# Retention and feed-forward kernel: the values of chunks 0 to 3 loaded through ScalarE's DMA queue, two casts placed earlier, and the last output block in one piece

## The chip, the core and the metric

The kernel runs on one core of a Trainium2 chip. The metric is the device time of one execution in microseconds (us), shorter being better. The core's engines are TensorE (PE in the profile, with its weight loads as PEld), VectorE (DVE), ScalarE (ACT), GpSimd (POOL) and SyncE (SP). Each works through its own list of instructions in order, and they meet through semaphores. Transfers between HBM and the on-chip memory are issued by an engine and carried out by 16 DMA engines.

## The reference

A retention layer with state (4 batches, 8 heads, 768 positions, head size 64) is followed by a feed-forward part without a nonlinearity. All inputs and the output are float32.

```python
gamma = 1.0 - 2.0 ** (-5.0 - np.arange(H))
for t in range(S):
    state = gamma * state + einsum('bhd,bhe->bhde', k[:, :, t], v[:, :, t])
    y[:, :, t] = scale * einsum('bhd,bhde->bhe', q[:, :, t], state)
x = y.transpose(0, 2, 1, 3).reshape(3072, 512)
h = ((x @ w1) * (x @ w2)) @ w3
out = h @ w_out
```

## The kernel before

**Tiling.** The 768 positions of a batch are cut into 6 chunks of 128, so there are 24 chunks, n = 0 to 23. A chunk's work is `casts(n)` on GpSimd (queries of a pair of chunks, keys, and values scaled into the buffer VP[n % 3], to float16), `transposes(n)` (keys transposed, on TensorE for early chunks), `scores(n)`, `kv(n)` (the state's update: a product on TensorE, an addition on VectorE, a decay on GpSimd at line 391) and `outputs(n)`, which uses the masked scores, VP and the state that `kv(n-1)` left. Its result is a piece of x. The feed-forward part works on blocks of at most 256 tokens of x: units "a" and "b" (x by w1 and w2) and "o" (the product by W3O). W3O = w3 by w_out is computed once at the start, since nothing stands between the two.

**Order of the work.** It is written by hand. A prologue loads w3 and w_out, transposes w3 block by block and builds W3O (lines 558 to 592), works on chunks 0 and 1 between (lines 583 to 598), casts w1 and w2 to float16 (lines 595 to 603, 631, 632), does the first block of tokens (lines 625 to 653), then chunks 2 and 3 (lines 666 to 682). From then on `step(n)` handles one chunk, and `fill.pull` puts feed-forward units between its parts (lines 519 to 540, 684 to 688). `step` calls `casts(n + 2)` ahead of the scores for n of 6 or more and behind `kv(n)` for n = 4 and 5.

**Loads.** All of them are issued by SyncE, through `dma_in` (line 62), in the order of lines 115 to 125: eight blocks for w3 and w_out, four more blocks of w3, the queries of chunks 0 and 1, keys and values of chunk 0, of chunk 1, four blocks of w1, four of w2, queries, keys and values of chunks 2 and 3, and the same of 4 and 5. A weight block or a pair's queries has 512 KB, a chunk's keys or values 256 KB in pieces of 256 bytes. Below, q0 stands for the queries of chunks 0 and 1, q2 for those of chunks 2 and 3, q4 for those of 4 and 5, k0 and v0 for the keys and values of chunk 0, and so on.

**Completion semaphores.** The framework has eight semaphores for such transfers (DMAHW0 to DMAHW7). It hands them out in turn, in the order in which the program's text issues the transfers, whichever engine issues them. Before an engine issues a transfer, it waits until the transfer that had the same semaphore last, eight places back in the text, has landed. Here is how the list of SyncE's instructions of this kernel shows it (rows 8 to 15 of the list):

```
8 L62 DMACopy stg<-in_moe_w_out_dram 128x1024
9 L62 DMACopy stg<-in_moe_w_dram 128x1024 [waits DMAHW0_49]
...
13 L62 DMACopy q_111<-in_q_dram 128x8x128 [waits DMAHW4_49]
14 L62 DMACopy k_113<-in_k_dram 128x8x64 [waits DMAHW5_49]
15 L62 DMACopy v_115<-in_v_dram 128x8x64 [waits DMAHW6_49]
```

**Stores.** `o_unit` (line 448) makes a block of 128 rows of the output: eight matmuls of 512 columns, one copy on ScalarE, one store by SyncE. The last block is made by `last_o_unit` (line 462) in two halves of 256 columns, each with its own copy and store.

Of the kernel before, what the change touches and what calls it, by code (L numbers as in the profile page):

```python
# [9 lines left out]
FP = mybir.dt.float32  # L10
HP = mybir.dt.float16
AF = mybir.ActivationFunctionType
# [6 lines left out]
def kernel(  # L19
# [11 lines left out]
    nc = tc.nc  # L31
    B, H, S, D = q.shape
    C = 128
    WST = 12
    NCH = S // C
    NSTEP = B * NCH
    NTOK = B * S
    DT0 = 8
    NP = H // 2
    DM = 512  # L40
    DFF = 1024

    final_scale = 1.0 / D
# [6 lines left out]
    ld = ctx.enter_context(tc.tile_pool(name="ld", bufs=6))  # L50
    att = ctx.enter_context(tc.tile_pool(name="att", bufs=2))
    fsb = ctx.enter_context(tc.tile_pool(name="fsb", bufs=2))
# [3 lines left out]
    ps_f = ctx.enter_context(tc.tile_pool(name="ps_f", bufs=3, space=PSUM))  # L56
# [4 lines left out]
    def dma_in(dst, src):  # L61
        nc.sync.dma_start(dst, src)  # L62

    chunk_in = {}
    q_in = {}

    def load_chunk(n):
        if n >= NSTEP:
            return
        b, c = divmod(n, NCH)  # L70
        tiles = []
        if c % 2 == 0:

            t = ld.tile([128, 2 * 512], FP, tag="q64", name="q64", bufs=3)
            dma_in(
                t[:, :].rearrange("p (h x) -> p h x", x=2 * D),
                q[b, :, c * C : (c + 2) * C, :].rearrange("h (p t) d -> p h (t d)", t=2),
            )
            q_in[n // 2] = t
        for nm, src in (("k", k), ("v", v)):  # L80
            t = ld.tile([128, 512], FP, tag=nm + "32", name=nm + "32")
            dma_in(
                t[:, :].rearrange("p (h d) -> p h d", d=D),
                src[b, :, c * C : (c + 1) * C, :].rearrange("h i d -> i h d"),
            )
            tiles.append(t)
        chunk_in[n] = tiles

    def new_stage():
# [56 lines left out]
    for h in range(H):  # L146
# [7 lines left out]
        out=keep[:, :], in_=keep[:, :], compare_op=mybir.AluOpType.is_ge, fill=0.0,  # L154
# [20 lines left out]
    for h in range(H):  # L175
        p, r = h // 2, (h % 2) * 64
# [9 lines left out]
    W3O = [wpool.tile([128, DM], HP, name=f"w3o_{i}") for i in range(8)]  # L186
# [3 lines left out]
    def cast_to(dst, src, on_dve):  # L190
        if on_dve:
            nc.vector.tensor_copy(dst, src)  # L192
        else:
            nc.scalar.copy(dst, src)  # L194
# [4 lines left out]
    def cast_w3(key, st):  # L199
        t = att.tile([128, 1024], HP, tag="w3h", name="w3h", bufs=4)  # L200
        cast_to(t[:, :], st[:, :], False)
        W3h[key] = t
# [22 lines left out]
    def w3_transpose(f):  # L225
        src, ps = w3_bank(f, f)
        for g in range(8):
            c0 = (g // 2) * 256 + g % 2
            nc.tensor.transpose(
                ps[:, g * 128 : (g + 1) * 128], src[:, c0 : c0 + 255 : 2], ident16[:, :]  # L230
            )
        w3_back(f, ps)

    def w3_mm_columns(i, acc, between=None):
        t = w3t.pop(("c", i))
        for f in range(4):
            if f == 2 and between:
                between()
            for r in range(2):
                g = f * 2 + r  # L240
                nc.tensor.matmul(
                    acc[f], lhsT=t[:, g * 128 : (g + 1) * 128], rhs=WO[i][:, r, :],
                    start=(i == 0 and r == 0), stop=(i == 3 and r == 1),
                )
            if i == 3:
                cast_to(W3O[f][:, :], acc[f], f < 3)
# [17 lines left out]
    def casts(n):  # L264
        if n >= NSTEP:
            return
        k32, v32 = chunk_in.pop(n)
        if n % 2 == 0:
            q16 = att.tile([128, 1024], HP, tag="q16", name="q16")
            nc.gpsimd.tensor_copy(  # L270
                q16[:, :].rearrange("i (t h d) -> i h t d", t=2, d=D),
                q_in.pop(n // 2)[:, :].rearrange("i (h t d) -> i h t d", t=2, d=D),
            )
            q16s[n // 2] = q16
        k16 = att.tile([128, 512], HP, tag="k16", name="k16", bufs=3)
        nc.gpsimd.tensor_copy(k16[:, :], k32[:, :])  # L276
        vp = VP[n % 3]

        for r in range(2):
            nc.gpsimd.tensor_tensor(  # L280
                vp[:, :, r, r * 64 : r * 64 + 64],
                v32[:, :].rearrange("j (p s e) -> j p s e", s=2, e=64)[:, :, r, :],
                VS[:, :].rearrange("j (p s) -> j p s", s=2)[:, :, r].unsqueeze(2).broadcast_to((128, NP, 64)),
                MULT,
            )
        k16s[n] = k16
# [30 lines left out]
    def dma_transposes(n):  # L317

        if n < DT0 or n >= NSTEP:
            return  # L320
        kT = att.tile([128, NP, 128], HP, tag="kT", name="kT", bufs=2)
        nc.sync.dma_start_transpose(kT[:, :, :], k16s[n][:, :])
        kTs[n] = kT
        if n % 2 == 0:
            qT = att.tile([128, 2, NP, 128], HP, tag="qTd", name="qTd", bufs=2)
            nc.sync.dma_start_transpose(
                qT[:, :, :, :].rearrange("p t a i -> p (t a) i"), q16s.pop(n // 2)[:, :]
            )
            qTd[n // 2] = qT
# [23 lines left out]
    def scores(n):  # L353
        kp = KP[n % 2]
        am = att.tile([128, NP, 2, 128], HP, tag="am", name="am")
        for half in range(2):
            ps = ps_at.tile([128, 2, 2, 128], FP, tag=f"psA{half}", name=f"psA{half}")
            for i in range(2):
                p = half * 2 + i
                for r in range(2):  # L360
                    nc.tensor.matmul(  # L361
                        ps[:, i, r, :], lhsT=kp[:, p, r, :], rhs=queries(n, p), start=True, stop=True
                    )
            nc.vector.tensor_tensor(  # L364
                am[:, half * 2 : half * 2 + 2, :, :].rearrange("j p s i -> j (p s) i"),
                ps[:, :, :, :].rearrange("j p s i -> j (p s) i"),
                keep[:, :].unsqueeze(1).broadcast_to((128, 4, 128)),
                MULT,
            )
        ATs[n] = am  # L370
# [44 lines left out]
    class Ffn:  # L415
# [43 lines left out]
            r0 = self.tok0 + tb * 128  # L459
            nc.sync.dma_start(out[r0 : r0 + 128, :], osb[:, :])  # L460

        def last_o_unit(self, tb):

            osb = fsb.tile([128, DM], FP, tag="osb", name="osb", bufs=3)
            r0 = self.tok0 + tb * 128
            for c in range(2):
                cs = slice(c * 256, c * 256 + 256)
                psO = ps_f.tile([128, 256], FP, tag="psF", name="psO")
                for f in range(8):
                    nc.tensor.matmul(  # L470
                        psO[:, :], lhsT=self.HT[:, f, tb * 128 : (tb + 1) * 128], rhs=W3O[f][:, cs],
                        start=(f == 0), stop=(f == 7),
                    )
                nc.scalar.activation(osb[:, cs], psO[:, :], AF.Copy, scale=final_scale)
                nc.sync.dma_start(out[r0 : r0 + 128, cs], osb[:, cs])

        def ab_units(self):
            need, m = self.tok0 + self.width, TB // self.width
            units = []
            for f in range(0, 8, m):  # L480
                units += [(need, 0.43, lambda f=f: self.a_unit(f)), (need, 0.43, lambda f=f: self.b_unit(f))]
            return units
# [32 lines left out]
    fill = Queue()  # L515
# [3 lines left out]
    def step(n):  # L519

        ready = n * C
        share = fill.available(ready) / (2 - n % 2)
        if n >= DT0 - 2:
            casts(n + 2)
        scores(n)
        fill.pull(share * 0.25, ready)
        t_new = kv(n)
        if n < DT0 - 2:
            casts(n + 2)
        dma_transposes(n + 2)  # L530
        if n == DT0 - 2:
            load_chunk(n + 4)
        if n % 2:
            q_transposes((n + 1) // 2)
        if n != 5:
            fill.pull(share * 0.25, ready)
        outputs(n)
        Tst[0] = t_new
        transposes(n + 1)
        fill.pull(share * (0.75 if n == 5 else 0.5), ready)  # L540

    def cast_w(W, st, d, on_dve):
        cast_to(W[d][:, :], st[d][:, :], on_dve)
# [29 lines left out]
    cast_wo(3)  # L573
    cast_w3(4, w3_st[4])
    cast_w3(5, w3_st[5])
    w3_mm_columns(3, acc)
    w3_transpose(4)
    w3_transpose(5)
# [19 lines left out]
    Tst[0] = kv(1)  # L598
    cast_w(W1, w1_st, 1, False)
    cast_w(W1, w1_st, 2, False)  # L600
    cast_w(W1, w1_st, 3, True)
    cast_w(W2, w2_st, 0, True)
    cast_w(W2, w2_st, 1, True)
# [2 lines left out]
    ffn = [Ffn(a, b - a) for a, b in zip(bounds, bounds[1:])]  # L606
    NT = len(ffn)
# [47 lines left out]
    for t in range(1, NT):  # L655
# [3 lines left out]
            fill.units += units[i : i + 8] + late[:1]  # L659
            late = late[1:]  # L660
        fill.units += late
    fill.units += ffn[NT - 1].o_units()[:-1]
    fill.units.append((0, 1.73, lambda: ffn[NT - 1].last_o_unit(ffn[NT - 1].width // 128 - 1)))


    load_chunk(6)
# [52 lines left out]
```

## Time and profile before

| | |
|---|---|
| times of three runs | 195.87, 196.1, 197.59 us (median 196.1) |
| time of the profiled execution | 196.1 us |
| its span (first to last instruction) | 194.2 us |
| granted TensorE clock, mean over the span | 0.999 |
| busy: TensorE, its weight loads, VectorE, ScalarE, GpSimd | 185.4, 140.4, 114.2, 97.3, 79.8 us |
| TensorE busy in 0 to 10, 10 to 20, 20 to 30, 30 to 40, 40 to 50 us | 7.58, 9.10, 9.64, 8.65, 9.39 us |
| TensorE busy in each later stretch, 60 to 190 us | all of it |
| DMA from 10 to 20, 20 to 30, 30 to 40 us | 384, 277, 357 GB/s |
| bytes moved by DMA | 40.15 MB, 39.86 MB of it on SyncE's queue |

How to read it: an engine's busy time is the time in which it had an instruction at work; matmuls overlap each other, so that TensorE can be "busy" without being at its peak. A group row or a wait row names the line of the kernel, what is written and read, how often, and what ended the engine's idle time. SPq is SyncE's instruction queue: the length of its DMA rows is the time that the issue took, not the transfer. The time from issue to landing is given apart, by line and tile.

### The profile page before, as it was taken

The page shows a single profiled execution, that of the slowest core. Times are in us where ns is not written, and L with a number is a line of the kernel's source. Part 1 is how long each engine was busy: PE and PEld are TensorE (multiplying, and loading weights), DVE is VectorE, ACT ScalarE, POOL GpSimd, SP SyncE. Part 2 cuts the span into 40 slices and gives each one's busy share as a digit, 9 for nine tenths or more (in the row PEclk, how much of TensorE's full clock was granted, in tenths as well). Part 3 has the DMA queues.
Part 4 walks back from the last instruction along what each step waited for, and adds up shares of the span by engine and source line. Part 5 has one row for each costly group of instructions (what it writes and reads, how often), then busy time and mean ns, then how long its engine had stood idle before and what let it go on. Part 6 is the DMA issues. An engine that isn't in the chain of part 4 may idle for free.

```text
span 194.2 us, 4673 instructions
## 1 busy us (share of the span) xinstructions
PE 185.4 (95%) x1781; PEld 140.4 (72%) x1781; DVE 114.2 (59%) x215; ACT 97.3 (50%) x189; POOL 79.8 (41%) x137
## 2 busy tenths in 40 slices
PE   6889996999999999999999999999999999999993
PEld 2435665757997889778877787788778877887752
DVE  3227367757877768657565666575657665753320
ACT  6478546336445453655545554555455545533322
POOL 7300362166977746386422643854226432200000
PEclk9999999999999999999999999999999999999999
DMA  6999999999999999999999989999999631111103
GB/s 201 372 391 387 228 310 405 344 205 239 287 212 238 171 262 218 224 217 250 189 193 236 194 191 173 235 219 191 189 243 214 137 95 21 59 54 54 46 28 146
DMA packets 87590, 40.15 MB, mean 207 GB/s; under 512 B 67984, under 2 KB 82576, under 8 KB 87568
## 3 DMA queue, kind: packets, MB, share of 16 engines
q1 hardware_dynamic: 87568, 39.86, 91.2%
q8 instruction: 14, 0.23, 0.5%
q14 instruction: 8, 0.07, 0.1%
HBM read 29.36 MB, written 6.29 MB: 184 GB/s over the span
## 4 chain that ended last, share of the span: by engine, by line
PE 82%; DMA 10%; ACT 2%; DVE 2%; SPq 1%; issue 1%; DVEq 0%
PE psF L427 39%; PE psO L453 21%; DMA stg<-in_moe_w_dram 10%; PE psA L361 6%; PE psW L254 3%; PE psY L400 2%; PE psY L399 2%; PE psY L402 2%; PE psK L382 2%; SPq L62 1%; PE psTq L302 1%; PE psO L470 1%; PE psT L348 1%; DVE w3o L192 1%; ACT w L194 1%
## 5 line engine op out<-in xcount | busy, mean ns | idle before, releaser
L427 PE MATMUL psF<-xt,w 128*128 128x256 f16 (+1 forms) x768 | 87.2, 264 | 0.0
L427 PEld LDWEIGHTS <-w 128*128 128x128 f16 x768 | 68.0, 98 | 6.8
L437 ACT COPY pa<-psF 128x256 f32<-128x256 f32 x88 | 32.7, 373 | 35.7 <-PE psF L427 35.2
L443 DVE TENSOR_TENSOR ht<-pa,psF 128x256 f16<-128x256 f32 x88 | 36.7, 417 | 23.3 <-PE psF L427 10.6
L364 DVE TENSOR_TENSOR am<-psA,keep 128x512 f16<-128x512 f32 x48 | 30.9, 685 | 22.9 <-PE psA L361 22.8
L453 PE MATMUL psO<-w3o,ht 128*128 128x512 f16 x184 | 43.6, 379 | 0.2 <-DVE ht L638 0.2
L391 POOL TENSOR_TENSOR t<-s,GS 128x512 f16<-128x512 f32 x16 | 20.7, 1295 | 45.8 <-DVE s L390 45.8
L280 POOL TENSOR_TENSOR vp<-v,VS 128x256 f16<-128x256 f32 x48 | 28.6, 618 | 12.5 <-PE psY L402 5.4
L453 PEld LDWEIGHTS <-ht 128*128 128x128 f16 x184 | 17.7, 98 | 17.4 <-DVE ht L638 1.0
L458 ACT ACTIVATE osb<-psO 128x512 f32<-128x512 f32 x23 | 13.7, 598 | 32.3 <-PE psO L453 32.3
L270 POOL CAST q<-q 128x1024 f16<-128x1024 f32 x12 | 12.5, 1038 | 21.0 <-DMA q<-in_q_dram 20.9
L407 DVE TENSOR_TENSOR xt<-psY,YS 128x512 f16<-128x512 f32 x24 | 17.7, 736 | 4.6 <-PE psY L402 3.4
L276 POOL CAST k<-k 128x512 f16<-128x512 f32 x24 | 14.7, 614 | 7.8 <-PE psK L382 7.0
L399 PE MATMUL psY<-am,vp 128*128 128x128 f16 x96 | 16.7, 219 | 1.0 <-DVE am L364 0.9
L400 PE MATMUL psY<-am,vp 128*128 128x128 f16 x96 | 16.7, 219 | 0.0
L361 PEld LDWEIGHTS <-kp 128*128 128x128 f16 x192 | 12.6, 98 | 5.5 <-ACT kp L194 0.7
L390 DVE TENSOR_TENSOR s<-psK,t 128x512 f32<-128x512 f32 x16 | 11.0, 689 | 3.3 <-PE psK L382 3.0
L212 DVE COPY w3t<-psW 128x1024 f16<-128x1024 f16 x8 | 5.5, 690 | 11.4 <-PE psW L220 8.1
L342 ACT COPY kp<-kT 64x512 f16<-64x512 f16 x16 | 9.9, 618 | 2.6 <-DMA kT<-k 2.2
L400 PEld LDWEIGHTS <-vp 128*128 128x128 f16 x96 | 9.4, 98 | 1.5 <-issue 1.2
L194 ACT CAST w3h<-stg 128x1024 f16<-128x1024 f32 x8 | 8.3, 1044 | 3.7 <-DMA stg<-in_moe_w_dram 3.7
L402 PE MATMUL psY<-qTd,t 128*128 128x128 f16 x56 | 10.1, 219 | 0.0
(69 smaller groups left out, 174.4 us busy)
## 6 DMA issues: line engine op xcount, KB each, us to landing
stg<-in_moe_w_dram SPq DMA_DIRECT2D x16, 512.0 KB, 8.3
q<-in_q_dram SPq DMA_DIRECT2D x12, 512.0 KB, 4.9
k<-in_k_dram SPq DMA_DIRECT2D x24, 256.0 KB, 5.3
v<-in_v_dram SPq DMA_DIRECT2D x24, 256.0 KB, 5.5
out_dram<-osb SPq DMA_DIRECT2D x23, 256.0 KB, 2.5
stg<-in_moe_w_out_dram SPq DMA_DIRECT2D x4, 512.0 KB, 7.7
kT<-k SPq DMA_TRANSPOSE x16, 4.5
out_dram<-osb SPq DMA_DIRECT2D x2, 128.0 KB, 1.7
```

The costliest lines, as they stand in the source:

```text
L276: nc.gpsimd.tensor_copy(k16[:, :], k32[:, :])
L280: nc.gpsimd.tensor_tensor(vp[:, :, r, r * 64 : r * 64 + 64], v32[:, :].rearrange("j (p s e) -> j p s e", s=2, e=64)[:, :, r, :], VS[:, :]. ...
L361: nc.tensor.matmul(ps[:, i, r, :], lhsT=kp[:, p, r, :], rhs=queries(n, p), start=True, stop=True)
L364: nc.vector.tensor_tensor(am[:, half * 2 : half * 2 + 2, :, :].rearrange("j p s i -> j (p s) i"), ps[:, :, :, :].rearrange("j p s i -> j ( ...
L391: nc.gpsimd.tensor_tensor(t16[:, :, :], s32[:, :, :], GS[:, :, :], MULT)
L399: nc.tensor.matmul(ps[:, p, :], lhsT=vp[:, p, 0, :], rhs=am[:, p, 0, :], start=True, stop=False)
L400: nc.tensor.matmul(ps[:, p, :], lhsT=vp[:, p, 1, :], rhs=am[:, p, 1, :], start=False, stop=(c == 0))
L407: nc.vector.tensor_tensor(XT[n // 2][:, :, n % 2 * C : (n % 2 + 1) * C].rearrange("p a (i t) -> p a t i", t=2), ps[:, :, :].rearrange(orde ...
L427: nc.tensor.matmul(ps[:, i * w : (i + 1) * w], lhsT=W[d][:, (f + i) * 128 : (f + i + 1) * 128], rhs=XT[self.tok0 // TB][:, d, c0 : c0 + w] ...
L437: nc.scalar.copy(self.pa[f][:, :], ps[:, :])
L443: nc.vector.tensor_tensor(self.HT[:, f : f + TB // self.width, :].rearrange("p f n -> p (f n)"), self.pa.pop(f)[:, :], ps[:, :], MULT,)
L453: nc.tensor.matmul(psO[:, :], lhsT=self.HT[:, f, tb * 128 : (tb + 1) * 128], rhs=W3O[f][:, :], start=(f == 0), stop=(f == 7),)
```

## The change

Three things are changed.

1. The values of chunks 0 to 3 are no longer loaded by SyncE in the order above. ScalarE issues them: v0 and v1 in the text behind the cast of w3's block 5, v2 and v3 behind ScalarE's casts of w1's blocks 1 and 2. All other loads stay with SyncE, in the old order without these four.
2. `step` calls `casts(n + 2)` ahead of the scores for every n, so also for n = 4 and 5 (chunks 6 and 7).
3. `last_o_unit` is gone: the last block is made by `o_unit` as all others are.

```diff
+    def load_kv(eng, nm, src, n):
+        b, c = divmod(n, NCH)
+        t = ld.tile([128, 512], FP, tag=nm + "32", name=nm + "32")
+        eng.dma_start(
+            t[:, :].rearrange("p (h d) -> p h d", d=D),
+            src[b, :, c * C : (c + 1) * C, :].rearrange("h i d -> i h d"),
+        )
+        return t
+
+    def load_v(n):
+        chunk_in[n].append(load_kv(nc.scalar, "v", v, n))
...
         for nm, src in (("k", k), ("v", v)):
-            t = ld.tile([128, 512], FP, tag=nm + "32", name=nm + "32")
-            dma_in(
...
-            tiles.append(t)
+            if nm == "v" and n < 4:
+                continue
+            tiles.append(load_kv(nc.sync, nm, src, n))
...
-        def last_o_unit(self, tb):
...
-        if n >= DT0 - 2:
-            casts(n + 2)
+        casts(n + 2)
         scores(n)
         fill.pull(share * 0.25, ready)
         t_new = kv(n)
-        if n < DT0 - 2:
-            casts(n + 2)
...
     cast_w3(4, w3_st[4])
     cast_w3(5, w3_st[5])
+    load_v(0)
+    load_v(1)
     w3_mm_columns(3, acc)
...
     cast_w(W1, w1_st, 1, False)
     cast_w(W1, w1_st, 2, False)
+    load_v(2)
+    load_v(3)
     cast_w(W1, w1_st, 3, True)
...
-    fill.units += ffn[NT - 1].o_units()[:-1]
-    fill.units.append((0, 1.73, lambda: ffn[NT - 1].last_o_unit(ffn[NT - 1].width // 128 - 1)))
+    fill.units += ffn[NT - 1].o_units()
```

More of the change, by code (lines that the diff above doesn't have):

```diff
@@ L80, in load_chunk @@
         for nm, src in (("k", k), ("v", v)):
-            t = ld.tile([128, 512], FP, tag=nm + "32", name=nm + "32")
-            dma_in(
-                t[:, :].rearrange("p (h d) -> p h d", d=D),
-                src[b, :, c * C : (c + 1) * C, :].rearrange("h i d -> i h d"),
-            )
-            tiles.append(t)
+            if nm == "v" and n < 4:
+                continue
+            tiles.append(load_kv(nc.sync, nm, src, n))
         chunk_in[n] = tiles
@@ L460, in o_unit @@
             nc.sync.dma_start(out[r0 : r0 + 128, :], osb[:, :])
-        def last_o_unit(self, tb):
[L464 to L475, printed above, removed]
         def ab_units(self):
```

## The prediction

> **What bounds the kernel now.** I read the page's busy times first, then the chain that ended last, then the timelines of the prologue by engine. TensorE carries the kernel:
>
> ```profile
> PE 185.4 (95%) x1781; PEld 140.4 (72%) x1781; DVE 114.2 (59%) x215; ACT 97.3 (50%) x189; POOL 79.8 (41%) x137
> PE   6889996999999999999999999999999999999993
> ```
>
> TensorE is idle for 8.8 us of 194.2. From 50 us on it hardly stops, so nothing there repays a delay: whatever the prologue loses, the end loses. The chain of waits, in order of time, shows the prologue:
>
> ```profile
> 19.12 1.90 PE psW L254 x8
> 21.02 0.45 PE psW L229 x8
> 21.47 1.73 PE psW L254 x8
> ...
> 26.71 0.86 PE psW L254 x4
> 27.57 0.14 PE psT L348 x3
> 27.71 10.48 DMA stg<-in_moe_w_dram
> 38.22 1.05 ACT w L194
> 39.32 0.41 PE psF L619 x2
> ```
>
> The 10.48 us of DMA look like a prize for any change that loads w2 sooner. They are not: TensorE's busy time is 8.65 us of the 10 from 30 to 40 us, so the last block of w2 came only a little after TensorE could have used it. Next ScalarE's timeline, where the change puts its new instructions (start, duration, idle time and its releaser):
>
> ```profile
> 17.35 1.05 ACT L194 CAST w3h<-stg 128x1024 f16<-128x1024 f32 x1 [0.24 <-DMA stg<-in_moe_w_dram]
> 18.30 0.58 ACT L194 CAST w3o<-psWy 128x512 f16<-128x512 f32 x1
> 18.78 1.05 ACT L194 CAST w3h<-stg 128x1024 f16<-128x1024 f32 x1
> 21.06 0.59 ACT L194 CAST w3o<-psW 128x512 f16<-128x512 f32 x1 [1.23 <-PE psW L254]
> ```
>
> Row one is the cast of w3's block 5. v0 and v1 are issued right behind it, ahead of rows two to four. Row three (block 6) is what TensorE's transposes at 21.02 read. Last SyncE's timeline and GpSimd's first use of q2:
>
> ```profile
> 10.64 0.38 SPq L62 DMA_DIRECT2D q<-in_q_dram  x1
> 11.93 4.02 SPq L62 DMA_DIRECT2D k<-in_k_dram  x1
> 16.00 3.68 SPq L62 DMA_DIRECT2D v<-in_v_dram  x1
> ...
> 28.45 0.43 SPq L62 DMA_DIRECT2D q<-in_q_dram  x1
> 29.42 4.95 SPq L62 DMA_DIRECT2D k<-in_k_dram  x1
> ```
>
> ```profile
> 39.93 1.04 POOL L270 CAST q<-q 128x1024 f16<-128x1024 f32 x1 [5.27 <-DMA q<-in_q_dram]
> ```
>
> Between q0's issue (done at 11.02) and k0's (11.93) SyncE waits, though nothing precedes k0. k0 shares its completion semaphore with the w_out block issued at 3.37, which landed 8.5 us later, at 11.87. So the wait for the transfer eight places back is real and holds the issuing engine.
>
> **What the change does to ScalarE.** The semaphores go round in the order of the text, and v0 now stands in the text behind every load of the list. The changed kernel's instruction list for ScalarE has:
>
> ```
> 13 L203 TensorCopy w3h<-stg 128x1024 [waits DMAHW1_49,PE_49,Activation_49]
> 14 L70 DMACopy v_333<-in_v_dram 128x8x64 [waits DMAHW7_49]
> 15 L70 DMACopy v_335<-in_v_dram 128x8x64 [waits DMAHW0_49]
> 16 L203 TensorCopy w3o_225<-psWy 128x512 [waits PE_49]
> 17 L203 TensorCopy w3h<-stg 128x1024 [waits DMAHW2_49,Activation_49]
> ```
>
> Counting loads in the text, the last one on DMAHW7 ahead of v0 is q2, and the last one on DMAHW0 ahead of v1 is k2. Both stand behind all eight blocks of w1 and w2. So ScalarE, free at 18.3, may not issue v0 until q2 has landed, nor v1 until k2 has. Queued behind it on ScalarE: the casts of W3O's blocks, of w3's blocks 6 and 7, the key copies, w1. TensorE stops at the transposes of block 6. SyncE is not held: what w1, w2 and q2 wait for on ScalarE are casts ahead of v0.
>
> Step by step (landings are the issue's start plus the time to landing that the view of line 62 gives for each transfer):
>
> - q2 lands. Before: 28.45 plus 11.4 to landing, 39.85. Two transfers leave the queue ahead of it. Neighbouring k and v landed 1.1 us apart (k1 at 25.8, v1 at 26.9), so 39.85 - 2 x 1.1 = 37.65. v0 landed 1.9 us behind k0, which makes it 36.9 if that much is saved once.
> - k2 lands. It followed q2 by 1.15 us before, so 38.8. v0 is then in flight on another queue of the same DMA engines. No row shows two such queues at once: between no sharing (0) and full sharing (1.1 us more), half, 39.35.
> - v1's issue on ScalarE. Nearest rows: SyncE's issues of keys or values in the steady part, 0.43 (a key) and 0.70 us (the value behind it); farthest, 4.02 and 4.95, when SyncE's queue was full. ScalarE's own queue is empty, so 0.70. ScalarE goes on at 40.05.
> - Its next two rows: the w3o cast (18.30 to the next start 18.78, 0.48), the cast of block 6 (1.05), and 0.05 to TensorE. The transposes start at 41.63 where they started at 21.02: **+20.6 us**, bounds 19.0 (k2 at 38.0, issue 0.43) and 24.5 (k2 at 39.9, issue 4.02).
> - TensorE restarts from some 20 us of idleness. The only other start from idleness is the first one: eight 512-column matmuls took 3.59 us (line 552), eight later ones 1.73 (the chain's row at 21.47). The chain is TensorE back to back for 6.7 us from 21.02, so a slow first 3.6 us costs 3.59 - 1.73, some **+1.8**. Bounds 0 (it stays fast) and 3 (it is slow for longer).
> - Gain behind it: all weights have landed by then (w2's last block at 38.2 - 2.2 = 36.0). Its cast at 38.22 could come 1.65 us sooner, when ScalarE is idle; but TensorE's preceding eight matmuls ran until 39.1 and the next started at 39.32: **-0.2**. GpSimd's casts of chunk 2 then run beside VectorE's casts, which could give it back: bounds -0.2 and +0.6.
> - v2 and v3: their semaphores' former transfers, k3 and q4, land about 40 to 42; ScalarE reaches them about 55. Two issues of 0.43 to 0.70 lie in the 3.0 us that ScalarE idled ahead of its copy at 35.50: 0; without that cover 0.9 to 1.4. Their data is wanted 13 us later; landing takes 5 to 6.
> - v0 and v1 land by about 45 (5.5 us from issue); with 1.19 us on GpSimd each they are ready by 46.2, and wanted at 26.49 + 22 and later: 0.
>
> The Trainium skill (page "DMA: Bandwidth & Descriptors", section "Issuing engines are not separate DMA queues") says that issuing from several engines saves only the issuing engine's own time. By it the move would be worth at most v0's and v1's 3.68 and 1.66 us of issue on SyncE, and the sum above without any hold would be about no change. For the restart, its page "TensorE: Matmul & The Clock Gate" says that about 3.4 us of idleness halves the clock until some 3.4 us have been busy again; by it the term would be an estimated 1.7 us. No run here shows a second cooling yet.
>
> **Casts of chunks 6 and 7 earlier.** Before, GpSimd did the decay of step 4's state at 55.04 (1.27 us) and then chunk 6's casts (1.04 + 0.62 + 1.20 = 2.9). Now the casts come first, at 53.7, if the loads are there. After the hold they are: SyncE has caught up. The decay then starts at about 56.6 and ends at 57.9; `outputs(5)` at 58.64 is its reader: 0. Bound +1.3, the decay's own length, if the casts start late. In step 5 there is no decay.
>
> **Last block.** Before: two ScalarE copies of 0.38, the last ending at 191.52, a store of 128 KB landing in 1.7. Now one copy of 0.60 and a store that lands in 2.0 as its neighbours: 0.22 + 0.3, matmuls 1.73 in place of 1.76: **+0.5**. SyncE issues one DMA fewer.
>
> Sum: 20.6 + 1.8 - 0.2 + 0.5 = 22.7. The profiled execution took 196.1 us (span 194.2 and 1.9 around it), equal to the median. Predicted: 196.1 + 22.7 = **218.8 us**.
>
> **The rivals.**
>
> - No hold: v0 and v1 are issued at 18.3 to 19.7, in the 1.23 us that ScalarE idles ahead of 21.06. Weights land 2.2 us sooner, worth 0.2; the tail costs 0.5: 196.4, not slower. It decides if q2 has landed by about 19.5. Against it: q2 stands behind 4 MB of weights, which took 11.3 us to land. Chance 0.04.
> - Issue itself stalls: ScalarE's issues, beside SyncE's full queue, take what SyncE's took, 4.95 and 3.49 us. Then 37.7 + 4.95 + 3.49 = 46.1 in place of 40.05: 225. For it: SyncE's queue is full just then. Against: the long rows were issues into the queue that was itself full. Chance 0.12, all outcomes above 222.5.
> - The queue drains faster and TensorE stays fast: with the other engines stopped, weights land at 1.25 us each as the first (26.9 to 28.15) and not 1.42, so q2 lands 1.4 us sooner; without the restart's 1.8: 215.6. Below 215: chance 0.08.
>
> **How the numbers follow.** The forecast, 215 to 222.5, has 0.74; the stall 0.12, shorter holds 0.08, no hold 0.04, more than one mishap 0.02. Least of all terms: 196.1 + 19.0 - 0.2 + 0.3 = 215.2; the most: 225 with the stalled issue. The range 215 to 225 holds 0.74 and most of the 0.12. One per cent, about 2 us, is what a measurement can tell here. Slower by over 1%: 0.96, all but the case of no hold; that one's 0.04 goes to within 1% (0.03) and faster (0.01).
>
> **What would show it.** ScalarE idle from 18.3 to about 38, ended by the DMA of q; TensorE idle from about 21 to 41; the first transposes and matmuls behind it at about twice 1.73 us per eight; v rows on ScalarE's queue, the first near 37.7, the pair v2 and v3 near 55 in idle time; from then on the old order, about 22 us later. It is wrong if the v0 row stands near 18.4.

## The result and the profile after

The changed kernel took 218.88 us (median of four runs, 217.63 to 219.49), against 196.57 us (median of four runs, 195.87 to 197.59) for the kernel before on the same chip: a ratio of 1.112, 95% interval 1.105 to 1.120. The prediction was 218.8, range 215 to 225. The profiled execution of the changed kernel took 219.49 us, its span 217.6 us (194.2 before).

The page of the changed kernel, busy times and slices of the span (40 of 5.4 us each):

```profile
PE 186.8 (86%) x1773; PEld 140.3 (64%) x1773; DVE 115.7 (53%) x215; ACT 97.1 (45%) x188; POOL 80.5 (37%) x137
...
PE   6788000497799999999999999999999999999993
...
PEclk9999755589999999999999999999999999999999
```

Every engine has the same work as before, within 1.5 us. What is new is a hole: three slices in which TensorE does nothing, and beside it a granted clock that falls to half.

ScalarE's timeline of the changed kernel, from the cast of w3's block 5 on, with the two DMA issues on its queue:

```profile
17.70 1.05 ACT L203 CAST w3h<-stg 128x1024 f16<-128x1024 f32 x1 [0.23 <-DMA stg<-in_moe_w_dram]
38.22 1.46 ACTq L70 DMA_DIRECT2D v<-in_v_dram  x2
39.72 0.58 ACT L203 CAST w3o<-psWy 128x512 f16<-128x512 f32 x1 [20.98 <-DMA k<-in_k_dram]
40.20 1.05 ACT L203 CAST w3h<-stg 128x1024 f16<-128x1024 f32 x1
41.15 0.59 ACT L203 CAST w3o<-psW 128x512 f16<-128x512 f32 x1
```

The four casts are the rows at 17.35, 18.30, 18.78 and 21.06 of before. The cast that followed at once now comes 20.98 us later, released by a transfer of keys. The row of the two v loads stands between. v0's issue began at 38.22: q2, issued by SyncE at 27.20, landed 11.0 us later, at 38.2. v1's began at 39.30, when k2 (27.96 and 11.3 us) had landed. TensorE's waits, and its timeline at the end of the hole:

```profile
PE psW L238 <- ACT w3h L203: 20.1, 2, 19.9
```

```profile
19.47 1.90 PE L263 MATMUL psW<-wo,w3t 128*128 128x512 f16 x8
41.30 1.04 PE L238 MATMUL psW<-ident,w3h 128*128 128x128 f16 x8 [19.93 <-ACT w3h L203]
42.13 3.47 PE L263 MATMUL psW<-wo,w3t 128*128 128x512 f16 x8
45.43 0.61 PE L238 MATMUL psW<-ident,w3h 128*128 128x128 f16 x8
45.88 0.61 PE L311 MATMUL psTq<-ident,q 128*128 128x128 f16 x8
46.33 0.39 PE L357 MATMUL psT<-ident,k 128*128 128x128 f16 x4
46.55 1.89 PE L263 MATMUL psW<-wo,w3t 128*128 128x512 f16 x8
```

The same eight matmuls of line 263 take 1.90, then 3.47 behind the hole, then 1.89 us again. The table of stretches gives for each stretch its length, the busy time (and instructions) of TensorE, its weight loads, VectorE, ScalarE and GpSimd, and then the granted clock, the DMA engines' share and GB/s:

```profile
20.00:25.00 5.00, 1.37 (x7) 0.40 (x5) 0.15 (x1) 0.00 (x0) 1.62 (x2) 0.98 1.18 258
25.00:30.00 5.00, 0.00 (x0) 0.00 (x0) 0.00 (x0) 0.00 (x0) 0.00 (x0) 0.50 0.95 356
...
35.00:40.00 5.00, 0.00 (x0) 0.00 (x0) 0.00 (x0) 0.28 (x1) 0.00 (x0) 0.50 0.92 202
40.00:45.00 5.00, 3.70 (x15) 1.90 (x16) 0.69 (x1) 2.68 (x4) 1.48 (x3) 0.50 1.33 249
45.00:50.00 5.00, 5.00 (x50) 3.30 (x49) 3.01 (x7) 1.75 (x3) 1.45 (x3) 0.97 0.84 132
```

The DMA engines work on through the hole; TensorE, VectorE and ScalarE stand still. The difference of the two spans, 23.4 us, can be laid out with four points of TensorE's work that both traces have (times before, then after; from the chain of waits, and for the fourth point from ScalarE's timeline, the row of the copy that ends the block before the last):

| stretch | before | after | longer by |
|---|---|---|---|
| start to the transposes of w3's block 6 | 21.02 | 41.30 | 20.28 |
| to the next transposes (block 7) | 23.20 | 45.60 | 2.12 |
| to the first block's output | 40.56 | 63.50 | 0.54 |
| to the copy that ends the block before the last | 189.39 | 212.33 | 0.00 |
| to the end of the span | 194.2 | 217.6 | 0.46 |

Of the 20.28, 0.35 lie ahead of the change: the cast of block 5 began at 17.70, not 17.35. In the profiled executions below that row starts between 17.13 and 18.56, whatever was changed, so this is the spread of the first loads.

The first two rows share a small shift. The chain lets the transposes of block 6 begin at 21.02, when the matmuls ahead of them had ended; the timeline of before has them at 20.86, and those of block 7 at 23.03. By the timelines of both kernels the first row is 20.44 us and the second 1.96 us.

### The profile page after: what moved, and what is told of

It reads as the page before. It is cut to its first block, busy times and chain, and to the rows that moved or that the text cites. A ratio compares the mean times of both kernels' runs of the same rounds, so it can differ in the third digit from the quotient of the medians.

```text
span 217.6 us, 4658 instructions
## 1 busy us (share of the span) xinstructions
PE 186.8 (86%) x1773; PEld 140.3 (64%) x1773; DVE 115.7 (53%) x215; ACT 97.1 (45%) x188; POOL 80.5 (37%) x137
## 4 chain that ended last, share of the span: by engine, by line
PE 74%; DMA 9%; SPq 8%; DVE 3%; issue 2%; ACT 1%; ACTq 0%; DVEq 0%
PE psF L436 35%; PE psO L462 19%; DMA k<-in_k_dram 5%; PE psA L370 5%; SPq L62 5%; DMA stg<-in_moe_w_out_dram 4%; SPq L70 4%; PE psW L263 3%; PE psY L408 2%; PE psY L409 2%; PE psY L411 2%; PE psK L391 2%; DVE w L201 1%; PE psF L614 1%; PE psTq L311 1%
## 5 line engine op out<-in xcount | busy, mean ns | idle before, releaser
L452 DVE TENSOR_TENSOR ht<-pa,psF 128x256 f16<-128x256 f32 x88 | 36.7, 417 | 22.7 <-PE psF L436 10.6
L462 PE MATMUL psO<-w3o,ht 128*128 128x512 f16 x192 | 45.4, 379 | 0.2 <-DVE ht L633 0.2
L462 PEld LDWEIGHTS <-ht 128*128 128x128 f16 x192 | 18.4, 98 | 18.4 <-DVE ht L633 1.0
L467 ACT ACTIVATE osb<-psO 128x512 f32<-128x512 f32 x24 | 14.3, 597 | 34.1 <-PE psO L462 34.1
L238 PE MATMUL psW<-ident,w3h 128*128 128x128 f16 x32 | 2.9, 242 | 20.1 <-ACT w3h L203 20.1
L285 POOL CAST k<-k 128x512 f16<-128x512 f32 x24 | 15.6, 649 | 7.3 <-PE psK L391 7.2
L238 PEld LDWEIGHTS <-w3h 128*128 128x128 f16 x32 | 2.3, 111 | 21.4 <-ACT w3h L203 20.8
```

Source lines behind the costliest of these rows:

```text
L452: nc.vector.tensor_tensor(self.HT[:, f : f + TB // self.width, :].rearrange("p f n -> p (f n)"), self.pa.pop(f)[:, :], ps[:, :], MULT,)
L462: nc.tensor.matmul(psO[:, :], lhsT=self.HT[:, f, tb * 128 : (tb + 1) * 128], rhs=W3O[f][:, :], start=(f == 0), stop=(f == 7),)
```

## The experiments

The theory is that the time goes into ScalarE's wait for a completion semaphore. The rivals are that ScalarE's queue, or two queues that share the DMA engines, cost the time; that the other two parts of the change have a share in it; and, for the 2.12 us, that the matmuls are slow for want of data and not for a slow clock.

**e1_no_hold.** Edit against the changed kernel:

```diff
-    w1_st = [load_rows(moe_w1, d) for d in range(4)]
-    w2_st = [load_rows(moe_w2, d) for d in range(4)]
-    for n in range(2, 6):
-        load_chunk(n)
...
     load_v(0)
     load_v(1)
+    w1_st = [load_rows(moe_w1, d) for d in range(4)]
+    w2_st = [load_rows(moe_w2, d) for d in range(4)]
+    load_chunk(2)
+    load_chunk(3)
...
     load_v(2)
     load_v(3)
+    load_chunk(4)
+    load_chunk(5)
```

In the built list (the instructions that the framework makes from the program's text), the order on each of the five engines is that of the changed kernel; only the semaphores, and with them the waits, differ. v0, v1 and v2 need no wait, v3 needs one.

> All parts of the change are kept, and so is the order of instructions on ScalarE; only the text that issues SyncE's later loads stands behind ScalarE's v loads, so that the v loads get semaphores whose former transfers land early. Theory (the hold on a completion semaphore is the loss): v0 and v1 are issued at 18.5 to 19.5 us, TensorE's transposes of w3's block 6 start at 20.9 to 21.5, the time is 196 to 198. Rival (ScalarE's queue itself, or two queues sharing the DMA engines, is the loss): the four v rows are still there, so 205 or more.

Measured: 198.93 us, ratio to before 1.011 (1.007 to 1.016). ScalarE's timeline of this kernel:

```profile
17.98 1.05 ACT L199 CAST w3h<-stg 128x1024 f16<-128x1024 f32 x1 [0.23 <-DMA stg<-in_moe_w_dram]
17.99 1.07 ACTq L70 DMA_DIRECT2D v<-in_v_dram  x2
19.10 0.59 ACT L199 CAST w3o<-psWy 128x512 f16<-128x512 f32 x1
```

Both v loads are issued within 1.07 us, on ScalarE's own queue, the transposes of block 6 start at 21.53, and 20 of the 22 us are gone. So it is not the queue that costs the 20 us; the wait does. The time is still 2.4 us above before and 0.9 above the upper end of what was expected. TensorE's waits of this kernel, and GpSimd's timeline, show what was not expected:

```profile
PE psT L353 <- POOL k L281: 1.9, 2, 0.9
```

```profile
28.52 0.61 POOL L281 CAST k<-k 128x512 f16<-128x512 f32 x1 [2.38 <-DMA k<-in_k_dram]
...
44.16 0.62 POOL L281 CAST k<-k 128x512 f16<-128x512 f32 x1 [0.95 <-DMA k<-in_k_dram]
```

k1 and k2 now land later than TensorE wants them (k1's cast started at 26.02 before, when nobody waited), at 0.94 us each. Two things can have moved them: v0 and v1 use the DMA engines ahead of k1, and SyncE's semaphores are shifted, so that k0 was issued at 15.35 where it was at 11.93. No run here separates the two. In the profiled executions, whose spans differ by 3.2 us, TensorE's waits for k1 and k2 are 1.9 us, the longer last block is 0.4 (from 192.18 to the end 5.22 us, 4.81 before), and the cast of block 5 began 0.6 later.

**e2_later_hold.** Edit against the changed kernel:

```diff
-    for n in range(2, 6):
+    for n in range(2, 4):
         load_chunk(n)
...
     load_v(0)
     load_v(1)
+    load_chunk(4)
+    load_chunk(5)
```

Again the order on all engines is that of the changed kernel. v0 and v1 get semaphores without a wait; v2 must wait for q2 and v3 for k2.

> Instructions stand on every engine in the order of the changed kernel; only the text of the loads of chunks 4 and 5 is moved, which gives v0 and v1 semaphores without a wait, while v2 must wait for q2 and v3 for k2. Theory: no hold at 18.3, but ScalarE, free at about 32.5, is held until k2 lands at about 41; its copies of the first block's product, at 35.5 before, start at 41 to 42, so 6 us later, with up to 1 us for a slower TensorE behind it and 0.5 for the last block: 201 to 204. Rival (the loss is the queue or its traffic): as the changed kernel, 217 to 220, or as the kernel before.

Measured: 203.7 us, ratio 1.037 (1.029 to 1.044). ScalarE's and TensorE's timelines of this kernel:

```profile
29.89 2.94 ACT L203 CAST w<-stg 128x1024 f16<-128x1024 f32 x3
39.33 1.37 ACTq L70 DMA_DIRECT2D v<-in_v_dram  x2
40.80 1.07 ACT L203 COPY stg<-psF 128x512 f32<-128x512 f32 x2 [7.97 <-DMA k<-in_k_dram]
```

```profile
41.44 1.07 PE L616 MATMUL psF<-xt,w 128*128 128x256 f16 x4 [4.23 <-ACT stg L203]
42.30 0.63 PE L616 MATMUL psYf<-xt,w 128*128 128x256 f16 x2
42.73 1.49 PE L616 MATMUL psF<-xt,w 128*128 128x256 f16 x6
```

The same mechanism in another place: held for 7.97 us, ScalarE costs TensorE only 4.23, since what stood behind the wait was not wanted at once. Its copies start at 40.80, a little ahead of the 41 to 42 expected. And 4.23 us of idleness are enough for a slow restart: six matmuls of 256 columns take 1.49 us where they took 0.82 before, and in stretches of half a microsecond the granted clock is 0.50 from about 40.4 to 47.2 us. From the first matmul behind the gap to the last pair of the block it is 5.87 us (41.44 to 47.31) where the same matmuls take 3.21 in e4 (57.97 to 61.18): 2.66 us, not the 1 us at most that was expected. With the 4.23 and 0.5 for the last block this makes 7.4 of the 7.5 us by which the span is longer.

**e3_hold_one_earlier.** Edit against the changed kernel: as e2, but only chunk 5's loads are moved behind `load_v(1)` (`range(2, 5)`, then `load_chunk(5)`). The order on all engines is unchanged; v1 waits for q2 in place of k2.

> As the changed kernel, but the text of chunk 5's loads stands behind v0's and v1's. v0 then waits for a block of w2 and v1 for q2, no longer q2 and k2. Theory: ScalarE goes on when q2 has landed and v1 is issued, about 1.1 us sooner than in the changed kernel (38.6 in place of 39.7), and the whole time is about 1 us less, 217 to 218.5. Rival: ScalarE's own issue sets the time: no change at 39.7.

Measured, one run: 218.42 us, span 216.6 (217.6 for the changed kernel). ScalarE's timeline:

```profile
34.70 3.57 ACTq L70 DMA_DIRECT2D v<-in_v_dram  x2
38.31 0.59 ACT L203 CAST w3o<-psWy 128x512 f16<-128x512 f32 x1 [19.13 <-DMA q<-in_q_dram]
```

v0's wait is over at 34.70, with a block of w2; ScalarE goes on at 38.31, 1.41 us sooner than in the changed kernel, released by q where it was k. The whole time cannot show 1 us in a single run; the trace does. The release follows the transfer that owns the semaphore.

**e4_kept_busy.** Edit against the changed kernel (84 matmuls whose results are not used; the rest of the computation is unchanged):

```diff
     w3_mm(4)
+    busy(84)
     w3_transpose(6)
```

> The changed kernel with 84 matmuls without use (512 columns) ahead of the transposes of w3's block 6, so that TensorE works through most of the hold. Theory (restart from idleness costs some 2 us): the eight matmuls behind the transposes take 1.73 us and not 3.3, and the time falls by 2.1 us, to 216 to 217.5. Rival (they are slow for another reason, such as data that comes late): 3.3 us again and the time as before, 218.5 to 219.5.

Measured: 217.28 us, ratio 1.104 (1.100 to 1.109); span 215.8. TensorE's timeline of this kernel:

```profile
22.07 18.29 PE L543 MATMUL psZ<-vp 128*128 128x512 f16 x84
41.52 0.62 PE L238 MATMUL psW<-ident,w3h 128*128 128x128 f16 x8 [1.16 <-ACT w3h L203]
41.98 1.89 PE L263 MATMUL psW<-wo,w3t 128*128 128x512 f16 x8
```

The matmuls behind the hold are back at 1.89 us for eight, with the same data and at almost the same time (41.98, and 42.13 in the changed kernel); the granted clock is 1.00 from 20 to 50 us. From the transposes of block 6 to the transposes of q it is 2.63 us here (41.52 to 44.15), 4.58 in the changed kernel (41.30 to 45.88), 2.62 before (20.86 to 23.48): the restart costs 1.95 us, and it comes from the idleness. The medians differ by 1.6, the spans by 1.8.

**e5_casts_only.** The kernel before with `casts(n + 2)` ahead of the scores for all n:

```diff
-        if n >= DT0 - 2:
-            casts(n + 2)
+        casts(n + 2)
         scores(n)
...
-        if n < DT0 - 2:
-            casts(n + 2)
```

> The kernel before with the second part of the change alone: casts of chunks 6 and 7 ahead of the scores of steps 4 and 5. Theory: here the hold does not give the loads time, so GpSimd waits for q6 (cast at 56.25 before, landing about 55) with the decay of step 4's state behind it; the decay then ends at 59 to 59.6 where outputs(5) wants it at 58.64: 0.4 to 1 us more, 197.0 to 197.6. Rival (the place of the casts does not matter at all): 196.6 and no wait of TensorE for line 391's decay.

Measured: 197.82 against 196.94 us, ratio 1.005 (1.002 to 1.007): 0.9 us, which is within the 0.4 to 1 us expected, though the time itself lies 0.2 above its range. GpSimd's timeline and TensorE's wait:

```profile
56.51 1.04 POOL L270 CAST q<-q 128x1024 f16<-128x1024 f32 x1 [1.42 <-DMA q<-in_q_dram]
...
60.07 1.26 POOL L391 TENSOR_TENSOR t<-s,GS 128x512 f16<-128x512 f32 x1
```

```profile
PE psY L402 <- POOL t L391: 1.1, 1, 1.1
```

The decay that ran at 55.04 now starts at 60.07, behind casts that waited for their load, and TensorE waits 1.1 us for it. The profiled execution is the slowest of the twelve (198.68 us): it also waited 1.2 us for the cast of w2's last block, so that step 4's last product on TensorE was already 1.4 us late (55.95 in place of 54.56). In the changed kernel this part costs nothing. There GpSimd's timeline has no wait ahead of these casts, and the decay follows in time:

```profile
76.56 1.05 POOL L279 CAST q<-q 128x1024 f16<-128x1024 f32 x1
...
79.27 1.28 POOL L400 TENSOR_TENSOR t<-s,GS 128x512 f16<-128x512 f32 x1
```

Nor does it cost anything in the profiled execution of e1, which has no hold: there chunk 6's casts start at 56.43 without a wait, the decay at 59.64, and TensorE's waits do not name it.

**e6_last_block_only.** The kernel before with the last block made by `o_unit`:

```diff
-    fill.units += ffn[NT - 1].o_units()[:-1]
-    fill.units.append((0, 1.73, lambda: ffn[NT - 1].last_o_unit(ffn[NT - 1].width // 128 - 1)))
+    fill.units += ffn[NT - 1].o_units()
```

> The kernel before with the third part alone: the last block in one piece. Theory: one copy of 0.60 in place of 0.38 behind the last matmul and a store that lands in 2.0 in place of 1.7: 0.5 us more, 197.1. The stretch from the last matmul's end to the end of the span is 0.5 us longer than before. Rival (one DMA and eight matmuls fewer win it back): 196.6 or less.

Measured: 197.06 against 196.94 us, ratio 1.001 (0.998 to 1.004): too little for the time to show. In the traces, from the start of the copy that ends the block before the last to the end of the span it takes 4.81 us before (189.39 to 194.2) and 5.25 here (190.15 to 195.4): 0.44 us.

## Why the prediction was right, point by point

- **The hold.** Predicted: q2 lands at 37.65, k2 at 39.35, ScalarE goes on at 40.05, the transposes start 20.6 us later. Measured: 38.2, 39.3, 39.72 and 20.28 (20.44 by the timelines), 0.35 of which lie ahead of the change. e1 and e2 have the same order of instructions on each engine and lose 2.4 and 7.1 us by the medians: that the semaphore's wait is the cause is shown.
- **The issue on ScalarE.** Taken as 0.70 us, measured 0.38 (v1's own issue in the chain of waits), while an issue of SyncE begun at 39.03 took 1.22. The rival of a stalled issue did not come about.
- **The restart.** Predicted 1.8, measured 2.12 by the chain, 1.96 by the timelines and 1.95 by e4. The granted clock fell at about 24.8 us, 3.5 us after TensorE's last matmul ahead of the hole, and in e2 at about 40.4, 3.2 us after. The Trainium skill's page "TensorE: Matmul & The Clock Gate" has the clock halved after some 3.4 us of idleness, and both agree. For the return the prediction took some 3.4 us of work from that page; here the clock came back 4.0 us after the first matmul behind the hole, and in e2 5.8 us after, which is why e2's restart cost 2.66 us. The measurement decides: the price of a restart is not one number.
- **The rest of the prologue.** Predicted -0.2, bounds -0.2 and +0.6: measured +0.54. The sign was wrong, the reason given for the upper bound fits: GpSimd has chunk 2's queries already and casts them (57.01, 1.50 us where it took 1.04) beside VectorE's casts, three of which take 3.80 us where they take 2.96 in e1, and TensorE waits 0.8 us for a copy of VectorE. That the one slows the other was not tried apart.
- **v2 and v3, v0's and v1's data.** Nothing, as predicted: v2's and v3's issues at 51.11 and 51.52 lie beside ScalarE's other work, and no wait of TensorE names the values.
- **The casts of chunks 6 and 7.** Nothing, as predicted; alone in the kernel before they cost 0.9 us (e5), because q6 had not landed. That it takes the hold to hide this is not shown: e1 has no hold and no such wait.
- **The last block.** Predicted 0.5, measured 0.46 in the changed kernel and 0.44 alone.
- **The sum.** 22.7 predicted; 23.4 in the profiled execution, 22.3 between the medians. That the two agree so closely is partly luck: the spread of the first loads alone is over 1 us, and the errors of the terms (0.3 too much for the hold, 0.3 and 0.7 too little for the restart and the rest of the prologue) partly cancel.

Two things in the prediction did not hold. The price of its rival without a hold, 196.4, was too low: e1 took 198.9, and its trace has TensorE waiting for k1 and k2; which of the two causes named above delayed them is open. The price also counted on weights that land 2.2 us sooner, and they did not: in e1 the last block of w2 was cast at 39.16, released by its load, where it was cast at 38.22 before, 0.3 us later even when the late start of 0.6 is taken off. The Trainium skill's page "DMA: Bandwidth & Descriptors" (section "Issuing engines are not separate DMA queues") says that issuing from a second engine saves no more than issuing time, and this agrees. And the rule that semaphores go round in the order of the text, which the description of the kernel before gives too, is too simple. In the changed kernel it gives the right answer, but in e2 v0's load stands in the text behind those of w1, w2 and chunks 2 and 3 and still comes ahead of q0 in the built list. The semaphores follow that list. In the list, v0's load comes behind v4's (e3) or v5's (the changed kernel) exactly when the text takes their buffers from the same pool first. That this is the framework's reason is argued from these lists, not shown.

No version here beats the kernel before.

## What to carry to other kernels

When a load is moved to an engine that also computes, look up in the built list what that load must wait for: a wait for an older transfer's semaphore stops everything queued behind it on that engine, and where the load stands among all loads decides which transfer it is. Here the engines' orders were equal to the last instruction, and the time went from 198.9 to 218.9 us by the waits alone. The price of one edit depends on what the others do to the same stretch (the casts: 0.9 us alone, nothing in the changed kernel and nothing seen in e1), so measure a part both alone and among the others.

## What the runs showed that had not been expected

- TensorE's clock was granted at 0.50 through a hole of 20 us; a gap of 4.23 us was enough to make the matmuls behind it slow (1.49 in place of 0.82 us for six) and cost more at the restart (2.66 us) than the hole did (1.95); 18.29 us of matmuls without use inside the hole bought the 1.95 us back.
- The first 18 us vary by more than 1 us from run to run (the cast of w3's block 5 starts between 17.13 and 18.56), nearly as wide as the spread of the changed kernel's four times (1.9 us).
- SyncE was not held by ScalarE: its loads went on through the hole, at 400 GB/s from 30 to 35 us. Behind the hole, up to 83 us, GpSimd's casts waited for a load only for v0 and v1 (at 43.52 and 46.25).
